# The last 128 dims of the first four x tiles: read as rows and turned on TensorE, in place of a transposing DMA

## The chip, the cores and the metric

The kernel runs on one core of one Trainium2 chip. The core has TensorE (PE: matmuls; PEld: its weight loads), VectorE (DVE), ScalarE (ACT), GpSimd (POOL) and SyncE (SP, which here only issues transfers), and 16 DMA engines that all transfers share. The metric is the device time of one execution in microseconds: 170.68 us is the median of 3 runs (170.39 to 171.07).

## What is computed

`x` is 2048 tokens of 448 dims, in bf16. The result is `g * a + (1 - g) * b`: a gated mix of a segmented attention with a memory (a) and of an MLP that mixes tokens (b).

```python
x = A_x                                                # (1, 2048, 448)
g = _sigmoid((x * gate_w).sum(-1, keepdims=True))
# a: 16 heads of 28 dims, 4 segments of 512 tokens
q, k, v = x @ wq, x @ wk, x @ wv
for s in range(4):
    logits = einsum('bhqd,bhkd->bhqk', qs, ks) * scale + mask
    a_dot = einsum('bhqk,bhkd->bhqd', softmax(logits), vs)
    a_mem = (phi(qs) @ M) / (phi(qs) @ z + 1e-06)      # phi(t) = t + 1 if t > 0 else exp(t)
    outs.append(sig(beta) * a_mem + (1 - sig(beta)) * a_dot)
    M, z = M + phi(ks).T @ vs, z + phi(ks).sum()
a = concat(outs) @ wo
# b: layernorm over dims, then a two-layer MLP along the token axis (2048 -> 1792 -> 2048)
h = layernorm(x)
u = gelu(einsum('bsd,sf->bdf', h, w1) + b1)
b = (einsum('bdf,fs->bds', u, w2) + b2).transpose(0, 2, 1)
return g * a + (1 - g) * b
```

## The kernel before

**x is held twice.** `xh` holds it as rows: 16 tiles of 128 tokens, 448 dims each, for the layernorm and, once normalised, as the moving operand of the MLP. `xT` holds it turned, with the dims on the partitions: 4 chunks of 128 dims by 2048 tokens, for the projections to q, k and v. The chunks begin at dims 0, 128, 256 and 320 (`C0`), so the third and the fourth overlap by 64 dims. `xT` comes from transposing DMAs on SP's queue: for each of four blocks of 512 tokens (`tc`) one transfer for chunks 0 to 2 (`dtx{tc}_0`) and one for chunk 3 (`dtx{tc}_1`). `xh` comes from four plain transfers of four tiles each (`ldx0`, `ldx4`, `ldx8`, `ldx12`).

**The projections come in pairs** (`pair`). A projection sums over the 448 dims: chunks 0, 1, and then chunk 2 and the upper half of chunk 3, or chunk 3 and the lower half of chunk 2. The two half chunks of a pair (64 rows each) go first, side by side in the array, in one operation `lo...`. For the first block of tokens the matmuls over chunks 0 and 1 are set apart as heads (`pra`, `prb`), so that they can run before chunks 2 and 3 are used.

**The order of the start, on TensorE:** nine warm-up matmuls (`warm`); a small transposition of the gate vector (`gtr`), which VectorE writes into a column of wv (`gw`); one more warm-up matmul; the eight heads of v of tiles 0 to 3 (`pra0` to `pra3` on chunk 0, `prb3` to `prb0` on chunk 1); the half chunks of v (`lot2`, `lot0`); the rest of v (`prt1`, `prt3`, `prt2`, `prt0`); the heads of k (`pra0_1` and on); and so on to the scores of the attention (`sc0_0`) and the MLP (`u`, `y`), which fill the rest of the run. VectorE copies the weights of k and q into padded form (`padk`, `padx`, `padq`, line 662) once they have landed, and empties some of the PSUM banks (`cpv`, `cpk`, `cpq`); ScalarE empties the others. `bns` (line 916) are the statistics of the layernorm.

**What sets the order:** `ORDER` is a table of names, one string for each engine; `Sched.plan` puts the operations on each engine in that order, and `Sched.finalize` makes semaphore waits of the dependences between them. Nothing moves at run time: an engine that waits holds up all that stands behind it on that engine. SP issues nearly all loads, one after another; ScalarE issues those of wv, of the last part of wk and a few small ones at the very start.

The line of the transposing DMA is 535, of the row loads 520, of the weight loads 525 and 529; 282 is the helper `mm` that issues the projections and the MLP, 973 the scores.

Of the kernel before, what the change touches and what calls it, by code (L numbers as in the profile page):

```python
# [297 lines left out]
def pool_cost(n):
# [6 lines left out]
    "PE": """  # L305
warm gtr@4 warm2 pra0@7 pra1@4 pra2@5 pra3@6 prb3 prb2 prb0 prb1 lot2 lot0 prt1 prt3 prt2 prt0 pra0_1 pra0_2 pra0_0
btr@7 lok0_0 lok0_2 prk0_0 prx0_3 prk0_2 prk0_1 prt7@4 prx1_3@5 prk1_2@6 lot6@7 lok1_2 loq0_0 loq0_2 prq0_2 prq0_0
prt6 prq1_2@4 prq0_2h prq1_1@5 prq1_2h@6 loq1_0@7 loq1_2 prq0_1 prq1_0 prk1_1@4 sc0_0 lok1_0@5 lot4@67 prk1_0 prt5
prt4 sc0_1 prk2_1@4 prx2_3@5 prk2_2@6 lok2_2 lok2_0@7 sc0_2 prk2_0 u1-0@6*5 u0-0@4 u1-5 u0-1*2 u2-0@5*3 sc0_3 u0-3
u2-3*2 u0-4*2 u3-0@7*2 u0-6 u2-5*2 u3-2 u1-6 sc0_4 u1-7 u0-7*6 u3-3 u0-13 u2-7 u3-4 u0-14*2 u1-8 sc1_0 u1-9*6 u2-8*2  # L310
u1-15 u2-10*4 u3-5*2 u4-0@4 u3-7*2 sc1_1 u5-0@6*2 u2-14 u5-2*2 u2-15 u3-9*6 u5-4 u3-15 u4-1*5 u5-5*2 pv1@5 u4-6*2
sc1_2 u4-8 u5-7*5 u4-9*4 u5-12 pv0@7 u5-13 sc1_3 u4-13*3 u6-0@5*3 u7-0@7 u6-3 u5-14 u6-4*2 u5-15 u6-6 sc1_4 u6-7
u7-1 u6-8*4 u7-2*2 u6-12 u7-4*3 u6-13*3 sc2_0 u7-7*7 pv2@4 u7-14*2 sc2_1 mst0@6 u8-0@4*2 prq2_1@5 prq2_0@7 loq2_0
sc2_2 u8-2*4 prq2_2@5 u8-6*4 prq2_2h@6 loq2_2 mem1 u8-10*2 u9-0@5 u8-12 u9-1*8 u8-13*2 u11-0@6 sc2_3 u9-9*3 pv3@7
u9-12 u8-15 u9-13*2 u11-1 u9-15 u11-2*4 sc2_4 u10-0@7*3 u11-6*6 u13-0@4 u10-3 pv4@5 sc3_0 u10-4*12 u11-12 u13-1
sc3_1 u13-2*3 u11-13*2 u13-5*2 pv5@5 u11-15 prt9@7 u13-7*4 sc3_2 lot8@5 u13-11*2 u12-0@6*5 prt8 u13-13*3 u12-5 sc3_3
lot10@57 u12-6*3 prt11 u12-9*7 prt10 sc3_4 mst1@7 prk3_1@4 pv6@6 prk3_0@7 lok3_0 sc4_0 prq3_1@5 prq3_0@7 wo0@6
loq3_0 lw0@4 sc4_1 wo1 pv7@5 prk3_2@6 wo3@7 lok3_2@4 lw2@5 sc4_2 wo2 prx3_3 y0-0@6*5 mem2 y0-5*9 prq3_2h@4 prq3_2@5
# [6 lines left out]
y10-10*2 y11-9*3 y10-12 y11-12*2 lw14@45 y10-13 wo14 wo15 wo12@7 y12-0@6*2 lw12@5 wo13 y13-0@4*4 y15-0@7 y13-4*2
y14-0@5*2 y13-6*4 y12-2 y14-2*2 y13-10 y14-4 y12-3*2 y13-11 y12-5*3 y14-5 y15-1 y12-8*3 y14-6*3 y13-12*2 y12-11*3
y14-9*5 y15-2*12 y15-0#1@4 y15-1#1 y15-2#1 y15-3#1 y15-4#1 y15-5#1 y15-6#1 y15-7#1 y15-8#1 y15-9#1 y15-10#1 y15-11#1
y15-12#1 y15-13#1""",
# [11 lines left out]
    "DVE": """  # L340
ob0 gw padk0 padx0 cpv3 padk1 padx1 padk2 padx2 padq0 padq1 b2c padq2 b1c padq3 cpk0_0 cpk0_2 mk0_0 bns3 bns1 bns0
phk0_0 bns2 bna1 bna3 bna2 bns7 bns9 bna0 bns5 bns10 vpe0 bns11 bns6 bna9 cpq1_0 bna7 bns4 bna6 gcol0 bna5 bna4 vpe4
nmr0 bna10 bns8 ln1 b1h ln2 bna8 cpk1_0 b1s mk0_1 bns13 bna11 phk0_1 nmr4 bns15 ln0 bna15 omgh vpe8 ln3 ln4 gh ln5
cpq2_3 bns12 bna12 bna13 bns14 ln6 mq1_1 bna14 nmr8 ln11 ln8 ln9 vpe12 ln10 ln7 omg0 nmr12 mg0 ln12 ln13 ln15 ln14
mq1_2 mg1 mg2 mo0 phq1_2 gvh0 garg0 phq1_1 garg1 mk0_2 gelu0 phk0_2 mq1_0 gvh2 gelu1 garg2 phq1_0 mk0_3 oc0 phk0_3
garg3 mq1_3 ta1 ta0 rec0 mk1_0 gelu2 oc1 gelu3 oa0 phk1_0 gvh5 gvh4 garg5 garg4 mk1_1 rec1 phk1_1 oa1 gelu4 gelu5
ta2 gvh6 gvh7 ot1 msta0 garg6 mstc0 mk1_2 phk1_2 rec2 phq1_3 garg7 cpq2_2 tm4 tm7 tm5 tm6 b2g0 eps6 gelu7 gelu6
mk1_3 eps4 phk1_3 oa2 ta3 mq2_0 phq2_0 gvh8 garg8 rec3 gcol1 eps7 garg9 mq2_2 ot2 ta4 gelu8 gelu9 rec4 ot0 oa3 omg1
mk2_0 mq2_1 phk2_0 phq2_1 garg10 ta5 gvh11 garg11 eps5 mk2_1 phk2_1 b2g1 om4 phq2_2 oa4 gelu11 ot3 gelu10 rec5 om5
gvh13 gvh12 msta1 garg12 oa5 garg13 ot4 ta6 cpk3_1 rec6 om6 ag0 oa6 ag1 ta7 gelu12 rec7 mq2_3 gelu13 phq2_3 mstc1  # L350
om7 oa7 tm8 tm9 tm10 tm11 cpq3_2 cpq3_2#1 ot5 mk2_2 eps8 eps9 eps11 gcol2 fin0 mk2_3 mq3_1 phk2_3 phk2_2 ta8 rec8
ot6 eps10 oa8 om8 ot7 phq3_1 oy8 fin1 fin3 ag4 ot8 mq3_0 phq3_0 ta9 rec9 omg2 fin2 om9 oa9 mq3_2 ta10 rec10 om10 ot9
ag7 fin5 mq3_3 phq3_2 oa10 ta11 rec11 msta2 phq3_3 oa11 mstc2 om11 tm12 tm13 tm14 tm15 ot11 ot10 cpv15 cpv14 eps13
fin4 ta12 eps15 gcol3 b2g2 eps12 omg3 rec12 oa12 fin6 ag8 om12 ta13 ot12 rec13 fin7 om13 oa13 o13 ot13 eps14 fin8
ag10 ta14 rec14 om14 oa14 ta15 rec15 om15 oa15 b2g3 fin9 ot14 ot15 fin11 fin10 fin13 fin12 fin14 fin15 fin15#1""",
# [23 lines left out]
def build_kernel(nc, X, WQ, WK, WV, WO, BETA, W1, B1, W2, B2, GW, OUT):  # L379
# [153 lines left out]
    def transpose_x(tc):  # L533
        for k, (c, n) in enumerate(((0, 3), (3, 1))):
            op("SP", lambda e, c=c, n=n: e.dma_start_transpose(
                xT[:, c : c + n, tc * 512 : tc * 512 + 512], x2[tc * 512 : tc * 512 + 512, C0[c] : C0[c] + 128 * n]),
               writes=[R_xT[tc][k]], name=f"dtx{tc}_{k}", dma=True, cost=1200 * n, nbytes=227000 * n, prio=(-3, -3, -1, 0)[tc])
# [294 lines left out]
    def do_gw():  # L832
        b = Bank()

        def gps():
            return bank(b)[:, 0:NCT]

        def fn(e):
            e.matmul(bank(b)[:, 0:3], gstage[:, :], ident[:, 0:5:2], start=True, stop=True, skip_group_check=True)
            return e.matmul(bank(b)[:, 3:4], gstage[:, :], ident[:, 5:6], start=True, stop=True, skip_group_check=True)  # L840
# [3 lines left out]
        op("DVE", lambda e: e.tensor_copy(wvx[:, :, D], gps()), use=(b,), reads=[bres(b)], writes=[R_gw], name="gw", cost=80,  # L844
           prio=P_BASE)
# [69 lines left out]
    def ln_stats(t):  # L915
        op("DVE", lambda e: e.bn_stats(st6[:, t, :], xh[:, t, :]), reads=[R_x[t]], writes=[R_st6[t]], name=f"bns{t}",  # L916
           cost=512, prio=P_PROJ - 10, rel=7500.0)
# [377 lines left out]
```

## Time and profile before

| | |
|---|---|
| median of 3 runs (range) | 170.68 us (170.39 to 171.07) |
| the profiled execution: its time; its span, first to last instruction | 170.68 us; 168.9 us |
| TensorE busy | 164.7 us (98%) |
| VectorE, ScalarE, GpSimd busy | 136.7 us (81%), 130.6 us (77%), 64.3 us (38%) |
| first matmul; first matmul of v; last matmul ends | 0.82; 5.21; in the microsecond from 166 to 167 |
| chain that ended last | TensorE 94%, a DMA 3% |
| DMA traffic | 25.44 MB, 151 GB/s mean |

A row of a timeline gives the start, the length and the engine, the line and the operation, out<-in, how many, and in brackets how long the engine had sat idle and what ended it. A matmul's record covers its whole way through the array; the next begins before it ends. So the spacing of the starts is what one costs. PEld rows show when the weights of a matmul are loaded, shortly before it starts. SPq and ACTq rows are the issue of transfers; the time to landing is counted from the start of the issue.

### The profile page before, as it was taken

The page shows a single profiled execution, that of the slowest core. Times are in us where ns is not written, and L with a number is a line of the kernel's source. Part 1 is how long each engine was busy: PE and PEld are TensorE (multiplying, and loading weights), DVE is VectorE, ACT ScalarE, POOL GpSimd, SP SyncE. Part 2 cuts the span into 40 slices and gives each one's busy share as a digit, 9 for nine tenths or more (in the row PEclk, how much of TensorE's full clock was granted, in tenths as well). Part 3 has the DMA queues.
Part 4 walks back from the last instruction along what each step waited for, and adds up shares of the span by engine and source line. Part 5 has one row for each costly group of instructions (what it writes and reads, how often), then busy time and mean ns, then how long its engine had stood idle before and what let it go on. Part 6 is the DMA issues. An engine that isn't in the chain of part 4 may idle for free.

```text
span 168.9 us, 4944 instructions
## 1 busy us (share of the span) xinstructions
PE 164.7 (98%) x2022; PEld 78.5 (47%) x2026; DVE 136.7 (81%) x321; ACT 130.6 (77%) x164; POOL 64.3 (38%) x100
## 2 busy tenths in 40 slices
PE   8999999999999999999999999999999999999994
PEld 2334444444554644544453454444454444564553
DVE  0088999877989989999999999999999978695042
ACT  0359999999999997999999998988985788604100
POOL 5000245260442524142177356445837355540000
PEclk9999999999999999999999999999999999999999
DMA  6998999888699945994337302328853129831202
GB/s 144 249 258 289 248 153 246 160 228 226 138 167 254 222 101 146 163 213 124 109 98 169 82 4 65 94 82 111 244 148 110 46 70 280 229 103 60 84 27 82
DMA packets 53974, 25.44 MB, mean 151 GB/s; under 512 B 18416, under 2 KB 53712, under 8 KB 53952
## 3 DMA queue, kind: packets, MB, share of 16 engines
q1 hardware_dynamic: 53160, 24.54, 61.2%
q10 hardware_dynamic: 792, 0.58, 1.7%
q8 instruction: 16, 0.26, 0.7%
q14 instruction: 6, 0.05, 0.1%
HBM read 18.82 MB, written 2.36 MB: 125 GB/s over the span
## 4 chain that ended last, share of the span: by engine, by line
PE 94%; DMA 3%; ACTq 1%; issue 1%; POOL 0%; DVE 0%; POOLq 0%
PE t L282 79%; PE t L973 8%; PE t L1003 5%; DMA t<-in_A_wv_dram 3%; PE t L856 1%; PE t L1076 1%; ACTq L525 1%; ACTq L546 0%; DVE t L1165 0%; POOL t L544 0%; POOL t L620 0%; POOL t L587 0%; POOL t L619 0%; POOL t L615 0%; POOLq L1280 0%
## 5 line engine op out<-in xcount | busy, mean ns | idle before, releaser
L282 PE MATMUL t<-t 128*32 128x448 bf16 (+9 forms) x1257 | 140.4, 352 | 1.0 <-issue 0.6
L282 PEld LDWEIGHTS t<-t 128*32 128x32 bf16 (+2 forms) x1261 | 63.7, 97 | 63.8 <-issue 15.3
L982 ACT ACTIVATE t<-t 128x2048 bf16<-128x2048 f32 x40 | 75.2, 1879 | 6.8 <-PE t L973 6.2
L985 POOL TENSOR_SCALAR_AFFINE_SELECT t<-t 128x512 bf16<-128x512 bf16 x64 | 43.3, 688 | 43.0 <-ACT t L982 40.0
L1040 POOL TENSOR_TENSOR t<-t 128x448 bf16<-128x448 f32 (+2 forms) x13 | 13.3, 1026 | 19.0 <-DVE t L1033 14.4
L1165 DVE SCALAR_TENSOR_TENSOR t<-t 128x448 bf16<-128x448 f32 (+2 forms) x17 | 10.7, 642 | 10.6 <-PE t L282 10.5
L973 PE MATMUL t<-t 28*128 28x512 bf16 (+3 forms) x256 | 15.8, 301 | 0.0
L1017 DVE STREAM_TRANSPOSE t<-t 128x512 f32<-128x512 f32 x16 | 11.3, 706 | 2.9 <-PE t L1003 2.7
L925 POOL TENSOR_TENSOR t<-t 128x4 f32<-128x4 f32 x4 | 4.2, 1054 | 23.4 <-DVE t L923 21.4
L1119 ACT ACTIVATE t<-t 128x448 bf16<-128x448 f32 x10 | 7.1, 732 | 7.6 <-PE t L282 7.6
L1003 PE MATMUL t<-t 128*32 128x512 bf16 (+3 forms) x256 | 11.5, 300 | 0.0
L1059 DVE STREAM_TRANSPOSE t<-t 128x512 bf16<-128x512 bf16 x16 | 10.9, 690 | 0.0
L973 PEld LDWEIGHTS t<-t 28*128 28x128 bf16 x256 | 4.4, 92 | 14.0 <-ACT t L982 7.7
L818 ACT ACTIVATE t<-t 128x448 bf16<-128x448 f32 x13 | 6.8, 546 | 4.2 <-PE t L282 4.2
L916 DVE BATCH_NORM_STATS2 t<-t 128x6 f32<-128x448 bf16 x16 | 9.3, 610 | 0.7 <-DMA t<-in_A_x_dram 0.7
L1145 DVE SCALAR_TENSOR_TENSOR t<-t 128x448 f32<-128x448 f32 x14 | 9.0, 649 | 0.7 <-ACT t L1140 0.6
L1003 PEld LDWEIGHTS t<-t 128*32 128x32 bf16 x256 | 6.7, 96 | 5.3 <-issue 0.7
L1137 ACT ACTIVATE t<-t 128x448 f32<-128x448 f32 x14 | 8.8, 638 | 0.1
L779 ACT ACTIVATE t<-t 128x512 bf16<-128x512 bf16 x12 | 7.6, 635 | 1.4 <-DVE t L736 1.4
L808 DVE SCALAR_TENSOR_TENSOR t<-t 128x512 bf16<-128x512 bf16 x12 | 8.5, 712 | 0.1
L1143 DVE TENSOR_SCALAR t<-t 128x448 f32<-128x448 f32 x10 | 6.5, 676 | 2.4 <-ACT t L1137 2.3
L1033 DVE SCALAR_TENSOR_TENSOR t<-t 128x448 f32<-128x448 f32 x12 | 8.4, 699 | 0.0
(76 smaller groups left out, 132.1 us busy)
## 6 DMA issues: line engine op xcount, KB each, us to landing
t<-in_B_w_dram SPq DMA_DIRECT2D x52, 256.0 KB, 3.9
t<-in_A_x_dram SPq DMA_DIRECT2D x4, 448.0 KB, 5.4
out_dram<-t SPq DMA_DIRECT2D x15, 112.0 KB, 2.0
t<-in_B_w_dram SPq DMA_DIRECT2D x8, 128.0 KB, 2.5
t<-in_A_wv_dram ACTq DMA_DIRECT2D x4, 112.0 KB, 4.1
t<-in_A_wq_dram SPq DMA_DIRECT2D x1, 336.0 KB, 4.8
spare_heads<-t SPq DMA_DIRECT2D x8, 32.0 KB
spare_heads<-t SPq DMA_DIRECT2D x16, 16.0 KB
```

The source lines that it names most:

```text
L282: last = e.matmul(out[q], w[:, q], x, skip_group_check=True, **kw)
L916: op("DVE", lambda e: e.bn_stats(st6[:, t, :], xh[:, t, :]), reads=[R_x[t]], writes=[R_st6[t]], name=f"bns{t}", cost=512, prio=P_PROJ - 10 ...
L973: last = e.matmul(bank(hl)[:, c0 : c0 + w], kT[r, hg, s * 512 + j * 128 : s * 512 + j * 128 + 128], qT[r, hg, s * 512 + 128 * j : s * 512 ...
L982: op("ACT", lambda e: e.activation(pslot(g), ps[:, 0:4, :], ACT.Exp, scale=SCALE), reads=R_bank[0:4], writes=[g.res], take=g, name=f"exp{p ...
L985: op("POOL", lambda e, c0=c0: e.affine_select(pslot(g)[:, :, c0 : c0 + 128], pslot(g)[:, :, c0 : c0 + 128], pattern=[[0, 4], [1, 128]], co ...
L1003: last = e.matmul(bank(cb)[32 * ((hl + hg) % 4) : 32 * ((hl + hg) % 4) + 32, 128 * j : 512], vaug[:, 4 * s + j, 32 * h : 32 * h + 32], psl ...
L1017: dv(lambda e: e.transpose(tt[:, ia, :], bank(cb)[:, 0:512]), [bres(cb)], [R_tt[ia]], "ta", 630, use=(cb,))
L1040: return e.tensor_tensor(dst, part(n3[0]), part(n3[1]), op=ALU.add)
L1059: dv(lambda e: e.transpose(oT[:, hg, s * 512 : s * 512 + 512], o), [R_ob[hg]] + ([R_obx] if hg else []), qres(hg, s), "ot", 635)
L1137: op("ACT", lambda e: e.activation(gg[:, q, :], bank(b)[:, 0:D], ACT.Square, bias=b1s[:, ft : ft + 1], scale=math.sqrt(GC)), **buse(b), re ...
L1145: op("DVE", lambda e: e.scalar_tensor_tensor(gg[:, q, :], gg[:, q, :], 1.0, vh[:, q, :], op0=ALU.add, op1=ALU.mult), reads=[R_gg[q], R_vh[ ...
L1165: op("DVE", lambda e: e.scalar_tensor_tensor(outst[:, p, c0:c1], bank(b)[:, 0 : c1 - c0], omg[:, T : T + 1], ag(T)[:, c0:c1], op0=ALU.mult ...
```

## The change

The transposing DMA of chunk 3 of the first 512 tokens (`dtx0_1`) is gone; those of the other blocks stay. In its place on SP's queue, right behind `dtx0_0`, a plain transfer `ldxl` reads dims 320 to 447 of the first four x tiles as rows into `xh` (128 partitions, 4 tiles, 128 dims: runs of 256 bytes), and `ldx0` later reads only dims 0 to 319. Four matmuls against the identity (`xtl`) turn the four 128x128 pieces into PSUM bank 2, and one copy on VectorE (`cpxl`, 128x512) writes them to `xT`. The statistics of tiles 0 to 3 now also wait for `ldxl`. What is computed is the same.

```diff
-dtx0_0 dtx0_1 ldwk0@0 ldwk1 ldwq0@1 ldwqb dtx1_0 dtx1_1 ldx0 ldx4 ldx8 ldbeta ldw1_0_0 dtx2_0 ldx12 dtx2_1 ldw1_0_1
+dtx0_0 ldxl ldwk0@0 ldwk1 ldwq0@1 ldwqb dtx1_0 dtx1_1 ldx0 ldx4 ldx8 ldbeta ldw1_0_0 dtx2_0 ldx12 dtx2_1 ldw1_0_1
...
+    R_xl = R("xl")
+
+    def load_x(eng, t0, n, c0=0, c1=D, writes=None, name=None):
+        op(eng, lambda e: e.dma_start(xh[:, t0 : t0 + n, c0:c1], xv[:, t0 : t0 + n, c0:c1]),
+           writes=writes or R_x[t0 : t0 + n], name=name or f"ldx{t0}", dma=True, cost=500, nbytes=n * 256 * (c1 - c0), prio=-3)
...
-        for k, (c, n) in enumerate(((0, 3), (3, 1))):
+        for k, (c, n) in enumerate(((0, 3), (3, 1))[: 2 if tc else 1]):
...
+    load_x("SP", 0, 4, C0[3], D, [R_xl], "ldxl")
     transpose_x(0)
...
-    load_x("SP", 0, 4)
+    load_x("SP", 0, 4, 0, C0[3])
...
+    def last_dims():
+        def fn(e):
+            for t in range(4):
+                last = e.matmul(bank(2)[:, t * 128 : t * 128 + 128], xh[:, t, C0[3] : D], ident[:, :], start=True, stop=True,
+                                skip_group_check=True)
+            return last
+
+        op("PE", fn, reads=[R_xl, R_ident], writes=[R_bank[2]], name="xtl", mode="f", cost=4 * pe_cost(128), prio=P_PROJ - 1)
+        op("DVE", lambda e: e.tensor_copy(xT[:, 3, 0:512], bank(2)[:, 0:512]), reads=[R_bank[2]], writes=[R_xT[0][1]],
+           name="cpxl", cost=dve_cost(512), prio=P_BASE)
```

The table of orders differs in little else: some bank numbers of the first v tiles, and a few neighbours exchanged further on. TensorE issues four matmuls more than before (2030 for 2026), which are those of `xtl`.

TensorE's start, before; "waits" names the semaphores (s_dma_u2 is that of `dtx0_1`, s_dma_u5 and s_dma_u6 those of the last two parts of wv; the second row of line 282 that has waits is `prb3`, the third `lot2`):

```order
L651 MATMUL t<-const-bfloat16-1.0 128x512
L282 MATMUL t<-t 128x449 [waits s_DVE,s_dma_u3,s_dma_u1]
L282 MATMUL t<-t 128x449 x3
L282 MATMUL t<-t 128x449 [waits s_dma_u4]
L282 MATMUL t<-t 128x449 x3
L282 MATMUL t<-t 128x449 [waits s_dma_u6,s_dma_u5,s_dma_u2]
L282 MATMUL t<-t 128x449 x7
L282 MATMUL t<-t 128x512 [waits s_DVE]
```

The same place of the changed kernel (s_dma_u1 is now `ldxl`):

```order
L282 MATMUL t<-t 128x449 [waits s_DVE,s_dma_u3,s_dma_u2]
L282 MATMUL t<-t 128x449 x3
L282 MATMUL t<-t 128x449 [waits s_dma_u4]
L282 MATMUL t<-t 128x449 x3
L854 MATMUL t<-t 128x128 [waits s_dma_u1]
L854 MATMUL t<-t 128x128 x3
L282 MATMUL t<-t 128x449 [waits s_dma_u6,s_dma_u5,s_DVE]
L282 MATMUL t<-t 128x449 x7
L282 MATMUL t<-t 128x512 [waits s_DVE]
```

The four turning matmuls stand behind the eight heads and before `lot2`; `lot2` no longer waits for a transposing DMA, but for VectorE, whose copy waits for these four.

VectorE's start, before (line 844 is `gw`, 662 the pads of k, 820 `cpv3`):

```order
L586 MEMSET t 128x256
L844 CAST t<-t 128x4 [waits s_PE]
L662 COPY t<-t 128x2x14x28 [waits s_dma_u7]
L662 COPY t<-t 128x2x14x4
L820 CAST t<-t 128x16x28 [waits s_PE]
```

And of the changed kernel (lines are shifted by 4; 859 is `cpxl`):

```order
L590 MEMSET t 128x256
L848 CAST t<-t 128x4 [waits s_PE]
L859 CAST t<-t 128x512 [waits s_PE]
L666 COPY t<-t 128x2x14x28 [waits s_dma_u7]
L666 COPY t<-t 128x2x14x4
L824 CAST t<-t 128x16x28 [waits s_PE]
```

The copy stands ahead of the first pads of k, which wait for the load of wk.

More of the change, by code (lines that the diff above doesn't have):

```diff
@@ L305 @@
     "PE": """
[L306 to L315, printed above, removed]
@@ L316 @@
-sc3_1 u13-2*3 u11-13*2 u13-5*2 pv5@5 u11-15 prt9@7 u13-7*4 sc3_2 lot8@5 u13-11*2 u12-0@6*5 prt8 u13-13*3 u12-5 sc3_3
-lot10@57 u12-6*3 prt11 u12-9*7 prt10 sc3_4 mst1@7 prk3_1@4 pv6@6 prk3_0@7 lok3_0 sc4_0 prq3_1@5 prq3_0@7 wo0@6
+warm gtr@4 warm2 pra0@5 pra1@4 pra2@6 pra3@7 prb3 prb2 prb0 prb1 xtl lot2 lot0 prt1 prt3 prt2 prt0 pra0_1 pra0_2
+pra0_0 btr@5 lok0_0 lok0_2 prk0_0 prx0_3 prk0_2 prk0_1 prt7@4 prx1_3@5 prk1_2@6 lot6@7 lok1_2 loq0_0 loq0_2 prq0_2
+prq0_0 prt6 prq1_2@4 prq0_2h prq1_1@5 prq1_2h@6 loq1_0@7 loq1_2 prq0_1 prq1_0 prk1_1@4 sc0_0 lok1_0@5 lot4@67 prk1_0
@@ new lines @@
+prt5 prt4 sc0_1 prk2_1@4 prx2_3@5 prk2_2@6 lok2_2 lok2_0@7 sc0_2 prk2_0 u1-0@6*5 u0-0@4 u1-5 u0-1*2 u2-0@5*3 sc0_3
+u0-3 u2-3*2 u0-4*2 u3-0@7*2 u0-6 u2-5*2 u3-2 u1-6 sc0_4 u1-7 u0-7*6 u3-3 u0-13 u2-7 u3-4 u0-14*2 u1-8 u2-8 sc1_0
+u1-9*6 u2-9 u1-15 u2-10*4 u3-5*2 u4-0@4 u3-7*2 sc1_1 u5-0@6*2 u2-14 u5-2*2 u2-15 u3-9*6 u5-4 u3-15 u4-1*5 u5-5*2
+pv1@5 u4-6*2 sc1_2 u4-8 u5-7*5 u4-9*4 u5-12 pv0@7 u5-13 sc1_3 u4-13*3 u6-0@5*3 u7-0@7 u6-3 u5-14 u6-4*3 u5-15 sc1_4
+u6-7 u7-1 u6-8*4 u7-2*2 u6-12 u7-4*3 u6-13*3 sc2_0 u7-7*7 pv2@4 u7-14*2 sc2_1 mst0@6 u8-0@4*2 prq2_1@5 prq2_0@7
@@ L324 @@
 y8-12*2 y9-4 sc7_4 lw10 y9-5*5 pv14@5 y10-0@6*7 y9-10*2 pv15@5 y11-0@7 y10-7 y11-1*3 y10-8*2 y9-12*2 y11-4*5
[L325 to L327 removed]
+y10-10*2 y11-9*3 y10-12 y11-12*2 lw14@45 y10-13 wo14 wo15 wo12@7 y12-0@6*2 lw12@5 wo13 y13-0@4*6 y14-0@5*2 y13-6*4
+y12-2 y15-0@7 y14-2*2 y13-10 y14-4 y12-3*2 y13-11 y12-5*3 y14-5 y15-1 y12-8*3 y14-6*3 y13-12*2 y12-11*3 y14-9*5
+y15-2*12 y15-0#1@4 y15-1#1 y15-2#1 y15-3#1 y15-4#1 y15-5#1 y15-6#1 y15-7#1 y15-8#1 y15-9#1 y15-10#1 y15-11#1
 y15-12#1 y15-13#1""",
@@ L340 @@
     "DVE": """
[L341 to L345, printed above, removed]
@@ L351 @@
[L351 to L355, printed above, removed]
+ob0 gw cpxl padk0 padx0 cpv3 padk1 padx1 padk2 padx2 padq0 padq1 b2c padq2 b1c padq3 cpk0_0 cpk0_2 mk0_0 bns3 bns1
@@ L356 @@
+rec8 ot6 eps10 oa8 om8 ot7 phq3_1 oy8 fin1 fin3 ag4 ot8 mq3_0 phq3_0 ta9 rec9 omg2 fin2 om9 oa9 mq3_2 ta10 rec10
+om10 ot9 ag7 fin5 mq3_3 phq3_2 oa10 ta11 rec11 msta2 phq3_3 oa11 mstc2 om11 tm12 tm13 tm14 tm15 ot11 ot10 cpv15
+cpv14 eps13 fin4 ta12 eps15 gcol3 b2g2 eps12 omg3 rec12 oa12 fin6 ag8 om12 ta13 ot12 rec13 fin7 om13 oa13 o13 ot13
+eps14 fin8 ag10 ta14 rec14 om14 oa14 ta15 rec15 om15 oa15 b2g3 fin9 ot14 ot15 fin11 fin10 fin13 fin12 fin14 fin15
+fin15#1""",
     "POOL": """
@@ L915, in ln_stats @@
     def ln_stats(t):
-        op("DVE", lambda e: e.bn_stats(st6[:, t, :], xh[:, t, :]), reads=[R_x[t]], writes=[R_st6[t]], name=f"bns{t}",
+        op("DVE", lambda e: e.bn_stats(st6[:, t, :], xh[:, t, :]), reads=[R_x[t]] + ([R_xl] if t < 4 else []), writes=[R_st6[t]], name=f"bns{t}",
            cost=512, prio=P_PROJ - 10, rel=7500.0)
@@ L1178, in build_kernel @@
     do_gw()
+    last_dims()
     def pairs(tc, *specs):
```

28 lines of the change are left out of this document (17 added, 11 removed).

## The prediction

> **What bounds the kernel now.** I read the page first, then busy time by stretches, then the chain of waits and the timelines of the first 12 us, then the transfers. The page says that TensorE is the bound, and the stretches say that it is so without a break:
>
> ```profile
> PE 164.7 (98%) x2022; PEld 78.5 (47%) x2026; DVE 136.7 (81%) x321; ACT 130.6 (77%) x164; POOL 64.3 (38%) x100
> PE 94%; DMA 3%; ACTq 1%; issue 1%; POOL 0%; DVE 0%; POOLq 0%
> ```
> ```profile
> 7.50:20.70 13.20, 13.12 (x75) 5.73 (x76) 10.95 (x34) 10.27 (x27) 1.04 (x1) 1.00 1.04 272
> 27.00:60.00 33.00, 33.00 (x473) 16.20 (x465) 28.86 (x72) 32.28 (x38) 13.88 (x21) 1.00 0.87 197
> 120.00:166.50 46.50, 46.50 (x605) 23.73 (x603) 33.03 (x63) 23.96 (x23) 17.57 (x24) 1.00 0.41 121
> ```
>
> The first busy time in a row is TensorE's: 13.12 of 13.20 us behind the start, 33.00 of 33.00, 46.50 of 46.50. So a microsecond that TensorE loses at the start comes out at the end, unless TensorE later loses one less somewhere else. The start in detail, by the chain of waits, then TensorE and its weight loads:
>
> ```profile
> 2.96 4.43 DMA t<-in_A_wv_dram
> 7.39 0.14 issue
> 7.52 1.42 PE t L282 x8
> ```
> ```profile
> 5.21 2.02 PE L282 MATMUL t<-t 128*128 128x449 bf16 x8
> 7.52 2.90 PE L282 MATMUL t<-t 64*128 64x449 bf16 x14 [0.29 <-DMA t<-in_A_wv_dram]
> ```
> ```profile
> 3.34 0.15 PEld L651 LDWEIGHTS t<-const-bfloat16-1.0 128*128 128x128 bf16 x1 [0.28 <-issue]
> 3.77 0.15 PEld L651 LDWEIGHTS t<-const-bfloat16-1.0 128*128 128x128 bf16 x1 [0.28 <-issue]
> ...
> 5.92 0.87 PEld L282 LDWEIGHTS t<-t 128*128 128x128 bf16 x5 [0.22 <-issue]
> 7.49 0.14 PEld L282 LDWEIGHTS t<-t 64*128 64x128 bf16 x4 [0.70 <-DMA t<-in_A_x_dram]
> 8.01 0.49 PEld L282 LDWEIGHTS t<-t 128*128 128x128 bf16 x4 [0.37 <-issue]
> 8.95 0.98 PEld L282 LDWEIGHTS t<-t 128*128 128x128 bf16 x6 [0.45 <-DVE t L662]
> ```
>
> The eight heads of v end at 5.21 + 2.02 = 7.23. `lot2` starts at 7.52, so the hole that the edit is about is 0.29 us wide. Two transfers end it nearly together. The chunk-3 transposition is issued at 2.24 (right behind the first one) and lands 5.0 later, at 7.24; the last part of wv is issued at 2.96 and lands 4.43 later, at 7.39:
>
> ```profile
> L535 SPq DMA_TRANSPOSE t<-in_A_x_dram x1: 1254/1254/1254, 2.2 to 2.2; - x1
> t<-in_A_x_dram SPq DMA_TRANSPOSE x1, 5.0
> t<-in_A_wk_dram SPq DMA_DIRECT2D x1, 224.0 KB, 4.9
> t<-in_A_wv_dram ACTq DMA_DIRECT2D x2, 112.0 KB, 4.5
> ```
>
> With the transposition away and the rest unmoved, `lot2` could not start before wv at 7.39: the wait that is removed is worth at most 0.29 us and, if wv lands as before, nothing.
>
> **What is removed.** One transposition of 1.25 us of SP's issue time; the row transfer in its place should take about what other plain ones do:
>
> ```profile
> 0.79 2.70 SPq L535 DMA_TRANSPOSE t<-in_A_x_dram  x2
> 3.55 1.08 SPq L525 DMA_DIRECT2D t<-in_A_wk_dram  x2
> 5.68 3.98 SPq L535 DMA_TRANSPOSE t<-in_A_x_dram  x2
> ```
>
> 1.08 / 2 = 0.54 us. So everything behind it on SP (wk, wq, the next transpositions, x rows, the first w1) is issued 1.25 - 0.54 = 0.7 us earlier. The traffic falls too: `ldx0` reads 128 KB less, just what `ldxl` reads, so the transposition's 128 KB are saved outright. Its packets run in the slices from 4 to 6 us, at the lowest rates of the start:
>
> ```profile
> DMA packets 1037, 0.29 MB, mean 290 GB/s; under 512 B 986, under 2 KB 1037, under 8 KB 1037
> DMA packets 290, 0.13 MB, mean 131 GB/s; under 512 B 195, under 2 KB 290, under 8 KB 290
> ```
>
> (The first row is the slice 3 to 4, the second 5 to 6.) I cost this relief at nothing by itself, since TensorE is full behind 7.5; it is only worth what it shortens waits, below.
>
> **When the rows land.** 128 KB, issued at about 2.24, 512 packets of 256 bytes behind the 1536 of the first transposition. At the 986 short packets per us of the slice 3 to 4 they take 0.5 us, at the 195 of the slice 5 to 6 they take 2.6 us. Counted from 4.0, where the first transposition's packets are about done, and with the 1.2 us from 6.0 to 7.24 that the removed one took from its last packets to its landing, that is 5.7 to 7.8. By the 4.5 us of 112 KB of wv it is 6.7. They are needed when the heads let go of the array, at 7.23 less the overlap of two matmuls. I take "in time"; the late end is a rival.
>
> The Trainium skill, "DMA: Bandwidth & Descriptors", Specifications, says that pieces under 512 bytes do not reach line rate, because a read-modify-write is done for them. The slice 3 to 4 speaks against a large effect here: 986 short packets went through at 290 GB/s, though for transposed data. By the page the 128 KB would cost like 256 KB or more, which is the late end again.
>
> **What is added in front of `lot2`.** Two steps that nothing covers, since `lot2` and all behind it wait on TensorE's one queue.
>
> ```profile
> L282 PE MATMUL t<-t 128*128 128x256 bf16 x12 | 1.8, 273 | 0.0
> L887 PE MATMUL t<-t 128*128 128x30 bf16 x1 | 0.2, 178 | 0.0
> L282 PEld LDWEIGHTS t<-t 128*128 128x128 bf16 x96 | 8.7, 98 | 11.0 <-issue 3.3 <-DVE t L662 0.4
> ```
> ```profile
> 4.89 0.18 DVE L844 CAST t<-t 128x4 bf16<-128x4 f32 x1 [3.71 <-PE t L840]
> 8.43 0.47 DVE L662 COPY t<-t 128x784 bf16<-128x784 bf16 x2 [3.36 <-DMA t<-in_A_wk_dram]
> 8.81 0.62 DVE L820 CAST t<-t 128x448 bf16<-128x448 f32 x1
> ...
> 11.33 0.69 DVE L736 CAST t<-t 128x512 bf16<-128x512 f32 x1
> ...
> 13.79 1.68 DVE L916 BATCH_NORM_STATS2 t<-t 128x6 f32<-128x448 bf16 x3 [0.70 <-DMA t<-in_A_x_dram]
> ```
>
> (1) The turning matmuls. Warm matmuls of 448 or 449 columns start 0.19 us apart (the five loads from 5.92 take 0.87), so the last head, whose record of 0.35 ends at 7.23, starts at 6.88 and the first `xtl` can start at 7.07. Four of 128 columns: below, four times 0.053 (512 columns cost 0.216 warm, a quarter is 0.054); above, four weight loads of 0.098. The last one's way through the array lies between the 0.178 of 30 columns and the 0.273 of 256: 0.22. The last ends between 7.45 and 7.58; I take 7.54. (2) The copy. A cast of 128x512 from PSUM takes 0.69. It starts 0.04 after the matmul (the small cast at 4.89, after a matmul that ends at 4.85), and a matmul's weight load follows a VectorE result by 0.11 (from 4.89 + 0.18 = 5.07 to the heads' first load at 5.18), the matmul itself by 0.03 more. So `lot2` starts at 7.54 + 0.04 + 0.69 + 0.14 = **8.41, 0.89 later than before** (0.80 to 0.93).
>
> **What is paid back.** First, at 8.95 the weight load for the heads of k waits for the pads of wk (0.45 before it, of which a spacing of 0.19 less a load of 0.10 is usual, and some is the four loads that came early). Without this wait the matmul would follow the last of v (8.01 + 0.03 + 4 x 0.19 = 8.80) instead of starting at 8.98: 0.18. In the changed kernel TensorE comes there at 9.69; wk, issued 0.7 earlier, lands by 8.45 - 0.7 = 7.75 and the pads (0.47) are done behind the copy at 8.27 + 0.47 = 8.74. So 0.18 comes back, 0.71 is left. VectorE's `cpv3` and the later pads move with TensorE, and stay as close to it as before. Second, at 24.16:
>
> ```profile
> 23.51 0.40 PE L973 MATMUL t<-t 28*128 28x384 bf16 x8
> 24.16 2.64 PE L282 MATMUL t<-t 128*128 128x512 bf16 x13 [0.26 <-issue]
> 26.73 0.40 PE L973 MATMUL t<-t 28*128 28x256 bf16 x8
> 27.07 3.09 PE L282 MATMUL t<-t 128*128 128x512 bf16 x15
> ```
> ```profile
> 18.10 1.18 SPq L535 DMA_TRANSPOSE t<-in_A_x_dram  x1
> t<-in_A_x_dram SPq DMA_TRANSPOSE x1, 6.0
> ```
>
> From scores to projections takes 27.07 - 26.73 = 0.34 where nothing is late, here 0.65: 0.31 is a wait, and it ends when the chunk-3 transposition of the third block lands (18.10 + 6.0 = 24.10). TensorE will come 0.7 later and that transfer not later than before, so this 0.31 comes back too. VectorE's own idle 0.70 before 13.79, for `ldx0`, takes up its lateness (the smaller `ldx0` is issued earlier). I find no other wait of TensorE for a load: 13.12 of 13.20 us are busy from 7.5 to 20.7, and none is left from 27 on.
>
> **Sum:** 0.89 - 0.18 - 0.31 = +0.40 us. The profiled execution took 170.68, which is also the median: **171.1 us**, +0.23%. A measurement here can tell about 0.5% (0.85 us) from no change, so this counts as the same.
>
> **Rivals.**
>
> (a) *The bubble stays whole.* If VectorE, with 10.95 us of work in 13.20, and the chain of bank releases behind it take the 0.89 without giving any back (the wait at 24.16 being that of an evacuation after all): 171.6, just past the 0.5%. For it: ScalarE and VectorE are nearly full from 22 to 60 us. Against it: the landing at 24.10 fits the start at 24.16 to a few hundredths. Decides: whether the pause before the projections at about 24.8 shrinks to 0.34.
>
> (b) *The rows land late* (slower). `ldxl` of short pieces lands after the heads, and `xtl` waits. It decides from a landing at 7.07 on, each 0.1 us later costing 0.1. The 256 KB loads of the same start are a bound:
>
> ```profile
> t<-in_B_w_dram SPq DMA_DIRECT2D x2, 256.0 KB, 5.8
> ```
>
> 2.24 + 5.8 = 8.04, 0.97 late: 171.08 + 0.97 = 172.0. Against it: at its place the queue carries only the first transposition.
>
> (c) *The pause drops TensorE's clock* (slower). The rows of the warm-up show it: loads 0.43 apart at 3.34 and 3.77 for 512 columns, against 0.216 later, so half speed. If a pause of 0.9 us sent it back for as long as the first ramp (0.82 to about 5.9, the heads from 5.92 being fast), half of 5 us is lost, 2.5: 173.6. A pause of 0.29 does nothing, by the spacing behind 8.01; none of 0.9 is in the trace. The Trainium skill, "TensorE: Matmul & The Clock Gate", What's actually happening, wants an idle window of about 3.4 us for that, which speaks against (c).
>
> (d) *The relief of the queues wins* (faster). Every load of the first 25 us comes 0.7 to 1.2 us earlier; if TensorE hides more waits for loads than its rows show, they come back. To be 0.5% faster, 0.89 + 0.85 = 1.7 us must be found, and the visible waits are 0.18 + 0.31; if as much again is hidden between records and 0.3 at each end, 170.3, still the same by the bound.
>
> (e) *The edit does nothing* because wv is last anyway: then no copy would be exposed, and 170.7. The order speaks against it: `lot2` waits for the copy.
>
> **Chances.** Forecast 0.57 (170.8 to 171.4); (a) 0.17, half of it past 0.5%; (b) 0.11; (c) 0.03; (d) 0.09, of which 0.05 past 0.5%; (e) 0.03. Slower: 0.085 + 0.11 + 0.03 = 0.23 with rounding; faster 0.05; same 0.72. The range from 170.3 to 171.9 takes in the forecast, (a), (e) and most of (d), and leaves out (b), (c) and the fast tail of (d).
>
> **What will show it.** In the changed profile: `xtl` (line 854) starting near 7.07 and not after a DMA; the cast of line 859 near 7.6, 0.69 long; the first 64-row matmul near 8.4 with VectorE as its releaser; the load for the heads of k 0.7 later than 8.95 and without a wait for line 666; the pause between scores and projections at about 24.9 at 0.34 instead of 0.65; and from there a constant lag of 0.4 to the end. It would be wrong if `xtl` waits for the x rows, if spacing behind 8.4 is 0.4, or if the lag at 27 is over 0.9 or below zero.

## The result, and the profile after

| | before | changed |
|---|---|---|
| median of 10 executions each (us) | 170.70 (170.12 to 171.07) | 171.46 (171.18 to 171.85) |
| ratio, with its 95% interval | | 1.0053 (1.0037 to 1.0068) |
| profiled execution: time / span (us) | 170.68 / 168.9 | 171.84 / 170.1 |

The change costs about half a per cent: the interval leaves out 1, and it lies across the 0.5% of the forecast. The median is 0.36 above the forecast of 171.1, inside the range of 170.3 to 171.9 and just outside the likeliest case's own range (170.8 to 171.4). The ten executions fall into two groups, six from 171.18 to 171.51 and four from 171.82 to 171.85. The profiled one is of the upper group; a second profiled execution of the same kernel, with a time like those of the lower group (171.43), stands below. Medians are over all executions of a run; ratios leave out the few in which the clock was visibly lower.

The summary of the page, after:

```profile
PE 164.2 (97%) x2026; PEld 78.5 (46%) x2030; DVE 137.4 (81%) x322; ACT 130.4 (77%) x164; POOL 63.7 (37%) x100
PE 93%; DMA 3%; SPq 1%; DVE 1%; issue 0%
```

TensorE is still the bound; what is new is that SP and VectorE stand in the chain. The chain of waits, after (start, length, what; two stretches of it):

```profile
2.21 5.66 DMA t<-in_A_x_dram
...
7.92 0.41 PE t L854 x4
...
8.35 0.70 DVE t L859
...
9.10 2.71 PE t L282 x14
...
11.87 2.51 PE t L282 x13
...
22.27 0.33 PE t L988 x4
...
25.01 0.33 PE t L988 x8
25.34 2.59 PE t L282 x13
...
149.63 18.07 PE t L282 x175
```

And the same places of the chain before, behind the rows that the prediction shows (wv landing at 7.39, `lot2` at 7.52):

```profile
10.43 2.73 PE t L282 x14
...
20.84 0.33 PE t L973 x4
...
23.58 0.33 PE t L973 x8
...
24.16 2.64 PE t L282 x13
...
148.46 18.07 PE t L282 x175
```

Read as lags of the changed kernel: `lot2` starts 9.10 - 7.52 = 1.58 later; the work behind its 14 matmuls 11.87 - 10.43 = 1.44 later; at 22.27 it is 1.43; at the projections 25.34 - 24.16 = 1.18; near the end 149.63 - 148.46 = 1.17, and the times differ by 171.84 - 170.68 = 1.16. So the whole loss arises ahead of `lot2`, 0.14 is paid back at the pads of k and 0.25 at the pause before the projections, and from there the lag is constant. That is the form that the forecast gave it. Its size at the start is not that of the forecast: 1.58 instead of 0.89.

TensorE's timeline at the start, after (the idle time before a row and what ended it stand in brackets):

```profile
4.93 1.68 PE L282 MATMUL t<-t 128*128 128x449 bf16 x8
7.92 0.40 PE L854 MATMUL t<-t 128*128 128x128 bf16 x4 [1.30 <-DMA t<-in_A_x_dram]
9.10 2.71 PE L282 MATMUL t<-t 64*128 64x449 bf16 x14 [0.79 <-DVE t L859]
```

The heads of v are done at 4.93 + 1.68 = 6.61, and TensorE then stands idle for 1.30 us until the x rows land at 2.21 + 5.66 = 7.87. The rows, not the heads, start the turning matmuls. In the second profiled execution, the chain of waits reads:

```profile
2.23 5.16 DMA t<-in_A_x_dram
...
7.43 0.41 PE t L854 x4
...
7.87 0.70 DVE t L859
...
8.62 2.72 PE t L282 x14
```

Here the rows land at 7.39, and `lot2` starts at 8.62. Both times `lot2` follows the landing by 1.23. The 0.48 between the two landings is close to the distance between these two times (171.84 - 171.43 = 0.41). That the landing makes the two groups is likely, but one profile of each doesn't show it. Finally two loads of the first profiled execution, one of wk issued at 2.84 and the last part of wv issued at 2.93 (KB each, us from issue to landing):

```profile
t<-in_A_wk_dram SPq DMA_DIRECT2D x1, 224.0 KB, 6.0
t<-in_A_wv_dram ACTq DMA_DIRECT2D x1, 112.0 KB, 5.1
```

Before, they took 4.9 and 4.43; in the second profiled execution of the change 5.2 and 5.0. So wk, though issued 0.7 earlier, lands at 2.84 + 6.0 = 8.84 here, later than the 3.55 + 4.9 = 8.45 of before. Which transfers slow each other down is tried below, by the run that holds back SP's later loads.

### The profile page after: what moved, and what is told of

Its sections match the earlier page's. It is cut to its first block, busy times and chain, and to the rows that moved or that the text cites. A ratio compares the mean times of both kernels' runs of the same rounds, so it can differ in the third digit from the quotient of the medians.

```text
span 170.1 us, 4953 instructions
## 1 busy us (share of the span) xinstructions
PE 164.2 (97%) x2026; PEld 78.5 (46%) x2030; DVE 137.4 (81%) x322; ACT 130.4 (77%) x164; POOL 63.7 (37%) x100
## 4 chain that ended last, share of the span: by engine, by line
PE 93%; DMA 3%; SPq 1%; DVE 1%; issue 0%
PE t L282 78%; PE t L988 8%; PE t L1018 5%; DMA t<-in_A_x_dram 3%; PE t L871 1%; SPq L538 1%; PE t L1091 1%; DVE t L859 0%; PE t L854 0%; DVE t L1180 0%; PE t L902 0%
## 5 line engine op out<-in xcount | busy, mean ns | idle before, releaser
L1000 POOL TENSOR_SCALAR_AFFINE_SELECT t<-t 128x512 bf16<-128x512 bf16 x64 | 42.8, 680 | 44.5 <-ACT t L997 41.5
L1160 DVE SCALAR_TENSOR_TENSOR t<-t 128x448 f32<-128x448 f32 x14 | 9.5, 682 | 0.8 <-ACT t L1155 0.7
L1048 DVE SCALAR_TENSOR_TENSOR t<-t 128x448 f32<-128x448 f32 x12 | 8.4, 698 | 0.0
L1165 DVE SCALAR_TENSOR_TENSOR t<-t 128x448 bf16<-128x448 f32 x14 | 8.4, 614 | 0.0
```

The costliest lines, as they stand in the source:

```text
L1000: op("POOL", lambda e, c0=c0: e.affine_select(pslot(g)[:, :, c0 : c0 + 128], pslot(g)[:, :, c0 : c0 + 128], pattern=[[0, 4], [1, 128]], co ...
L1160: op("DVE", lambda e: e.scalar_tensor_tensor(gg[:, q, :], gg[:, q, :], 1.0, vh[:, q, :], op0=ALU.add, op1=ALU.mult), reads=[R_gg[q], R_vh[ ...
```

## One number that orders all runs

In all but three of the profiled executions, the span less the start of `lot2` is nearly the same:

| kernel | `lot2` | span | difference |
|---|---|---|---|
| before | 7.52 | 168.9 | 161.4 |
| changed, the two profiled executions | 9.10, 8.62 | 170.1, 169.6 | 161.0, 161.0 |
| e1 (rows loaded, nothing turned), e5 (nothing loaded), e9 (identity turned) | 7.76, 8.03, 7.90 | 168.7, 169.0, 168.9 | 160.9, 161.0, 161.0 |
| e3 (chain alone), e8 (rows on ACT) | 8.07, 9.15 | 169.1, 170.2 | 161.0, 161.1 |
| e11 (other transposition earlier) | 7.46 | 168.4 | 160.9 |

So an experiment on the start can be read from one row, the start of `lot2`, plus 161.0; the kernel before alone carries 0.4 more, which any later start gets back. The spans are given to 0.1. The three that don't follow are e2 (rows first on SP) and e4 (whole rows), where TensorE ran at half speed, and e10, where later loads were held back. A profiled execution need not be a typical one: that of e9 is the fastest of its twelve, and that of e5 is 0.43 slower than its median.

## The experiments

The theory behind them: the loss has two parts, the chain of four matmuls, a copy and two handovers that nothing covers (the forecast's +0.4), and rows that land too late (rival b). The rivals to it: that the chain itself costs more than forecast, that the earlier loads on SP cost time, and that the transposition taken away was worth something.

**The chain alone.** The kernel before, with all transfers as they were; four matmuls of the identity and a 128x512 copy into memory that nothing uses yet, which `lot2` waits for.

```diff
+        op("PE", fn, reads=[R_ident], writes=[R_bank[2]], name="xtl", ...)
+        op("DVE", lambda e: e.tensor_copy(uT[:, 0:2, 0:256], bank(2)[:, 0:512].rearrange("p (a b) -> p a b", a=2)),
+           reads=[R_bank[2]], writes=[R_scr, R_uT[0], R_uT[1]], name="cpxl", ...)
-                 x=..., need=rx + R_wv + [R_gw],
+                 x=..., need=rx + R_wv + [R_gw] + ([R_scr] if t < 4 else []),
```

> The kernel before with its chunk-3 transposition kept, plus four 128x128 matmuls of the identity and a copy of 128x512 on VectorE that lot2 waits for, so that only the turning and the copy are added and no transfer is changed; the copy's result is not used. Theory: lot2 at 8.41 (0.89 later), 0.18 and 0.31 come back, lag 0.40: 171.1. Rival (bubble stays whole): 171.6. Rival (the turning costs nothing and the transfers are all of it): 170.7.

171.07 against 170.73, ratio 1.0020 (1.0006 to 1.0033). TensorE's timeline of this kernel:

```profile
5.21 1.75 PE L282 MATMUL t<-t 128*128 128x449 bf16 x8
6.80 0.39 PE L851 MATMUL t<-t 128*128 128x128 bf16 x4
8.07 2.72 PE L282 MATMUL t<-t 64*128 64x449 bf16 x14 [0.88 <-DVE t L856]
```

`lot2` starts 1.27 after the first turning matmul (forecast 8.41 - 7.07 = 1.34), and the kernel loses 0.34 (forecast 0.40). The chain is what the forecast said it is, and it is less than half of the 0.76 between the two medians of the change.

**The change without its wait for the rows.** As the changed kernel, rows loaded at the same place, but the turning matmuls read the identity instead of them and wait for no transfer; the last 128 dims of the first 512 tokens are so left out of the computation.

```diff
-                last = e.matmul(bank(2)[...], xh[:, t, C0[3] : D], ident[:, :], ...)
+                last = e.matmul(bank(2)[...], ident[:, :], ident[:, :], ...)
-        op("PE", fn, reads=[R_xl, R_ident], ...)
+        op("PE", fn, reads=[R_ident], ...)
```

> The changed kernel with all its transfers, but the four matmuls turn the identity, which is there from the start, and not the rows: they don't wait for the row load, so chunk 3 of the first 512 tokens holds ones and zeros and not x. It takes the landing of the rows out of the chain and leaves the turning and the copy in. Theory (the forecast's chain of 0.4 plus about 0.4 for rows that land after the heads): 171.0 to 171.1, lot2 at 8.0 to 8.1 or with wv if that is later. Rival (earlier issue of the other loads costs the extra 0.4, whatever the rows do): 171.4 to 171.5.

170.96 against 170.64 for the kernel before on the same chip, ratio 1.0018 (1.0004 to 1.0032). Its chain of waits:

```profile
6.85 0.24 PE t L854 x4
7.11 0.70 DVE t L859
...
7.90 2.72 PE t L282 x14
```

The changed kernel again, on this chip:

> The changed kernel once more, beside the others on the same chip: 171.3 to 171.6. Theory: the rows land at another time in this execution (in the kernel without turning they landed at 7.2 behind the same transfers, against 7.87 here before), and the start of lot2 follows the landing by 1.2.

171.32, ratio 1.0045 (1.0029 to 1.0061). So with the rows' transfer running but not waited for, the loss is 0.32, near the chain's 0.34; with the wait it is 0.68. **The lateness of the rows is worth 0.36**, on the same chip and with the same transfers. The chain measured by itself and this lateness add up to 0.34 + 0.36 = 0.70, against 0.76 between the medians of the change.

**Neither chain nor transposition.** Two kernels leave the last 128 dims of the first 512 tokens at zero: one keeps the changed kernel's transfers, rows among them, the other is the kernel before with the transposition dropped and nothing in its place.

```diff
-... prb2 prb0 prb1 xtl lot2 lot0 ...
+... prb2 prb0 prb1 lot2 lot0 ...
-        op("DVE", lambda e: e.tensor_copy(xT[:, 3, 0:512], bank(2)[:, 0:512]), reads=[R_bank[2]], ...)
+        op("DVE", lambda e: e.memset(xT[:, 3, 0:512].bitcast(U32), 0), ...)
```

> The changed kernel with its row load, but without the four turning matmuls and their copy: chunk 3 of the first 512 tokens is set to zero on VectorE ahead of the gate column, so this part of x does not enter q, k and v of these tokens. Theory (the loss is the exposed chain of landing, turning and copy): lot2 starts when wv lands, and that is 7.4 to 8.05; time 170.4 to 171.0, clearly below the 171.46 of the changed kernel. Rival (the loss is on the transfer side: wv and wk land later since SP issues its loads earlier): lot2 at 8.05 or later behind wv, wk waits grow too, 171.2 to 171.5.

```diff
-dtx0_0 dtx0_1 ldwk0@0 ldwk1 ldwq0@1 ldwqb ...
+dtx0_0 ldwk0@0 ldwk1 ldwq0@1 ldwqb ...
+    op("DVE", lambda e: e.memset(xT[:, 3, 0:512].bitcast(U32), 0), writes=[R_xT[0][1]], name="cpxl", ...)
```

> The kernel before without the chunk-3 transposition of the first 512 tokens and with nothing in its place: that part of xT is set to zero on VectorE at the start, so these 128 dims do not enter q, k and v of these tokens. It bounds what the removal can be worth. Theory: lot2 waits for wv alone, at 7.1 to 7.4, worth 0 to 0.3 us: 170.4 to 170.7. Rival (the relief of the queues is worth more): 169.8 to 170.2.

The first takes 170.62, ratio 0.9992 (0.9981 to 1.0002); the second 170.40, ratio 0.9989 (0.9975 to 1.0002). Neither can be told from before. Why, the chains of waits say, the first kernel's

```profile
2.93 4.70 DMA t<-in_A_wv_dram
...
7.76 2.72 PE t L282 x14
```

and the second's:

```profile
2.96 4.93 DMA t<-in_A_wv_dram
...
8.03 2.72 PE t L282 x14
```

With nothing left to wait for but wv, `lot2` starts at 7.76 and 8.03, later than the 7.52 of before. The last part of wv is issued at 2.93 to 2.96 as ever, but takes 4.70 and 4.93 instead of 4.43: wk and wq are issued earlier on SP, and the run with SP's loads held back, below, shows that this counts. In the second kernel's profiled execution `lot2` is therefore 0.5 later, of which the 0.4 above comes back. Its median execution is 0.43 faster; by the 161.0 of the table its `lot2` would start near 7.6 (an estimate). So the wait that the edit removes was worth little: the intervals leave room for a gain of 0.2 to 0.25%, 0.3 to 0.4 us, and for none, and the forecast's own bound was "at most 0.29 us and, if wv lands as before, nothing".

The slice from 5 to 6 us of the second kernel:

```profile
DMA packets 359, 0.29 MB, mean 290 GB/s; under 512 B 35, under 2 KB 359, under 8 KB 359
```

Before, this slice had 131 GB/s; in the run with the chain alone, which keeps the transposition, it has 141.

**SP's later loads held back.** The changed kernel, in which the first load of wk, and so everything behind it on SP, waits until the rows have landed.

```diff
-               writes=[r[k]], name=f"ld{name}{k}", ...)
+               reads=[R_xl] if name == "wk" and k == 0 else [], writes=[r[k]], name=f"ld{name}{k}", ...)
```

> The changed kernel, but SP issues wk and all that stands behind it only when the rows have landed, so that the rows share the DMA engines with the first transposition and ScalarE's small loads and wv alone. It will be slower as a whole (wk lands some 5 us later than before, near 12); what counts is when the rows and wv land. Theory (the rows are late because the DMA engines stand half idle for about 1 us behind the transposition): landing still 7.0 to 7.9, with the slice 4 to 5 us still under 220 GB/s. Rival (the rows and wv are late because wk and wq, issued 0.7 us earlier, take their share): rows by 6.5 and the last part of wv by 6.8.

The last part of wv and the rows in this kernel:

```profile
t<-in_A_wv_dram ACTq DMA_DIRECT2D x1, 112.0 KB, 3.9
t<-in_A_x_dram SPq DMA_DIRECT2D x1, 128.0 KB, 4.5
```

The rows land 4.53 after their issue instead of 5.16 to 5.66, at 6.74, and the last part of wv at 2.93 + 3.9 = 6.83 instead of about 8. So what SP issues right behind the rows (wk, wq, then the next transpositions) delays both by 0.6 to 1.2 (one profiled execution); which of these loads does it is not separated. Of the two expectations it is the rival's that comes near (6.5 and 6.8). Here the rows are in time, and the heads, which end at 7.62, hold back the turning: `lot2` starts at 8.63, no earlier than in the second profiled execution of the change. The kernel takes 172.19, ratio 1.0088 (1.007 to 1.0107; two executions), because wq then comes late:

```profile
8.18 3.71 DMA t<-in_A_wq_dram
...
12.35 2.36 PE t L282 x11
```

The Trainium skill, "DMA: Bandwidth & Descriptors", Issuing engines are not separate DMA queues, says that transfers share the same 16 DMA engines and interleave, whichever engine issued them. These rows agree: what SP issues moves the landing of what ACT issued.

**Another place for the rows.** `ldxl` first on SP, ahead of the transposition:

```diff
-dtx0_0 ldxl ldwk0@0 ...
+ldxl dtx0_0 ldwk0@0 ...
```

> The changed kernel with the row load issued ahead of the transposition of chunks 0 to 2 on SP. Theory (the rows land at 7.87 because they stand behind that transposition): they land near 3.1 (issue at 0.79 plus the 2.3 of the first wv part), the turning starts when the heads let go, the heads start up to 0.6 later (5.2 to 5.5); lot2 8.4 to 8.7, the lag from 26 us on 0.4 to 0.7, time 171.0 to 171.3. Rival (short 256-byte pieces are slow wherever they stand): landing 5.7 us behind the issue, 6.5, and the first transposition 1 us or more later, heads at 6 or later: 171.6 to 172.2.

177.62, ratio 1.0368 (1.0326 to 1.0411): both expectations fell, the slower one by over 5 us. The transfers issued up to 5 us, then the chain of waits, then the weight loads:

```profile
t<-in_A_x_dram SPq DMA_DIRECT2D x1, 128.0 KB, 2.9
t<-in_A_x_dram SPq DMA_TRANSPOSE x1, 7.0
```
```profile
1.31 7.03 DMA t<-in_A_x_dram
...
8.38 3.18 PE t L282 x8
...
12.78 4.58 PE t L282 x14
```
```profile
9.11 0.15 PEld L282 LDWEIGHTS t<-t 128*128 128x128 bf16 x1 [0.23 <-issue]
9.48 0.15 PEld L282 LDWEIGHTS t<-t 128*128 128x128 bf16 x1 [0.22 <-issue]
```

The rows themselves are there early, 2.9 after issue, where 112 KB of wv issued at the same time took 2.4. So the 256-byte pieces alone don't account for the 5.2 and 5.7 of the change. But the transposition behind them takes 7.0 to land, where it took 3.7 to 3.9 as the first on the queue. The heads start at 8.38, and TensorE runs them at half speed: loads 0.37 apart for 449 columns, which take 0.19 in the forecast's rows, and the 14 matmuls of `lot2` take 4.58 instead of 2.72.

The rows on ACT's queue ahead of the last parts of wv, and turned between the two halves of the heads, where the copy is covered:

```diff
-ldwv0 ldgw ldwv1 ldwv2 ...
+ldwv0 ldgw ldxl ldwv1 ldwv2 ...
-... pra3@7 prb3 prb2 prb0 prb1 xtl lot2 ...
+... pra3@7 xtl prb3 prb2 prb0 prb1 lot2 ...
-dtx0_0 ldxl ldwk0@0 ...
+dtx0_0 ldwk0@0 ...
```

> The changed kernel with the row load issued by ScalarE between the gate vector and the second part of wv, and the turning matmuls put between the heads on chunk 0 and those on chunk 1, so that the copy runs beside the latter. Theory (the exposed chain is the loss): the copy is hidden, lot2 waits for the last part of wv, issued 0.5 later than in the changed kernel and landing near 8.2; 170.6 to 171.0. Rival (the row load on ScalarE's queue delays the second part of wv by 0.5 or more and with it the heads): 171.2 to 171.6. Rival (a plain transfer ahead of or beside the first transposition slows that, as when the rows were first on SP): heads at 6 or later, over 172.

171.91, ratio 1.0083 (1.0063 to 1.0103), 0.9 above the 170.6 to 171.0 that the theory gave. Its chain of waits:

```profile
3.50 5.52 DMA t<-in_A_wv_dram
...
9.15 2.72 PE t L282 x14
```

The rows land 4.5 after an issue at 1.97, at 6.47; turning and copy are done well before wv lands and cost nothing. But wv's last part is issued at 3.50 instead of 2.93 and takes 5.52 instead of 4.43, and `lot2` is as late as in the slower profiled execution of the change. The chain can be hidden, and then wv decides.

**The rows as whole rows.** `ldxl` reads all 896 bytes of each row at the same place, 448 KB, and the later `ldx0` goes:

```diff
-    load_x("SP", 0, 4, C0[3], D, [R_xl], "ldxl")
+    load_x("SP", 0, 4, 0, D, [R_xl] + R_x[0:4], "ldxl")
-    load_x("SP", 0, 4, 0, C0[3])
```

> The changed kernel with whole rows of the first four tiles (896-byte pieces, 448 KB) loaded at the place of the 256-byte pieces (128 KB), and no later load of their other dims. Theory A (the pieces are late since they are short): as many pieces, each at line rate, land no later than 7.4, and the time falls to 171.0 to 171.2. Theory B (they are late since everything behind the transposition waits for a gap in which the DMA engines are half idle, and then goes by its bytes): the landing moves to 8.2 to 8.8, time 171.8 to 172.3.

173.97, ratio 1.0192 (1.0158 to 1.0227). Chain of waits, the transfers of the slice 4 to 5, and busy time by stretches (TensorE, weight loads, VectorE, ScalarE, GpSimd, then the granted clock, the DMA share and GB/s):

```profile
2.22 6.61 DMA t<-in_A_x_dram
...
8.87 0.41 PE t L853 x4
...
10.05 4.19 PE t L282 x14
```
```profile
DMA packets 173, 0.14 MB, mean 136 GB/s; under 512 B 23, under 2 KB 173, under 8 KB 173
```
```profile
9.00:10.00 1.00, 0.27 (x4) 0.09 (x2) 0.69 (x2) 0.00 (x0) 0.00 (x0) 0.88 1.61 310
11.00:12.00 1.00, 1.00 (x3) 0.34 (x4) 0.12 (x1) 0.00 (x0) 0.00 (x0) 0.50 1.11 244
13.00:14.00 1.00, 1.00 (x6) 0.39 (x4) 0.23 (x3) 0.97 (x6) 0.00 (x0) 0.91 0.68 154
```

Two things. The slice 4 to 5 has a low rate with almost no short pieces (23 of 173 packets under 512 bytes, 136 GB/s; before, it had 189). And the rows land 6.61 after issue, at 8.83, just past the range of theory B; the time is over its range because of the clock. TensorE waits 1.44 and then 0.78 for the copy, and its clock is granted at 0.50 from 10 to 13. Taken from the 0.88 and the 0.91 of the rows at both ends, half speed lasted from about 9.76 to 13.18, that is 3.4 us (an estimate). This is rival (c), seen after a longer pause than that of the change.

**The other wait alone.** The kernel before, with the third block's second transposition issued before the load of the x rows of tiles 12 to 15, so that it lands ahead of the projections that wait for it:

```diff
-... ldw1_0_0 dtx2_0 ldx12 dtx2_1 ldw1_0_1
+... ldw1_0_0 dtx2_0 dtx2_1 ldx12 ldw1_0_1
```

> The kernel before, with the chunk-3 transposition of the third block issued ahead of the last load of x rows and not behind it. It tests the second payback: if TensorE's pause before the projections at 24.16 was a wait for that landing, it goes: 23.9 instead of 24.16, and the kernel is 0.2 to 0.3 us faster than before (170.4). Rival (the pause has another cause, a bank that is let go late): no change, 24.16 and 170.65; or a loss, if the last tiles' statistics, now 0.6 us later, hold VectorE up.

170.37 against 170.75, ratio **0.9976 (0.9957 to 0.9994)**. The chain of waits:

```profile
7.46 2.77 PE t L282 x14
...
23.40 0.33 PE t L973 x8
23.73 2.59 PE t L282 x13
```

From these scores to the projections it is 23.73 - 23.40 = 0.33; before it was 24.16 - 23.58 = 0.58 in the same view. The pause that pays back part of every later start is a wait for this transposition, and it can be had without losing anything first. This kernel is faster than both: 0.4 below before on the same chip, and about 1.1 below the 171.46 of the changed one.

## Why the prediction came out as it did

It was right on the sign, on where the time is lost (TensorE's queue ahead of `lot2`) and on where it is paid back. Its sum was 0.36 short, mainly through one term, the landing of the rows. One of its own signs of being wrong came: `xtl` waits for the x rows. The lag at 27 (28.31 - 27.13 = 1.18 in the first profiled execution, 0.70 in the second) is over its bound of 0.9 in the first.

The accounts of the two profiled executions close: the turning starts 0.85 and 0.36 later than the 7.07 of the forecast, the chain behind it is 0.16 and 0.15 shorter than its 1.34, and 0.10 less is paid back. That makes 0.79 and 0.31 on top of the 0.40, and the measured lags near the end are 1.17 and 0.72.

- **"I take 'in time'"** for the landing of the rows is the step that failed. The forecast's own range for the landing was 5.7 to 7.8; measured are 7.39 and 7.87, at its late end and just past it, against the 7.07 at which they were needed, and the 6.7 by which it judged them. Rival (b), given 0.11, is what happened, at a smaller price than its 172.0: each 0.1 of lateness did cost 0.1, and the lateness was 0.3 to 0.8. The removed transposition took 5.0 to its landing; the rows in its place take 5.0 to 5.7 in the four profiled executions with these same transfers (the change twice, e1, e9). That 512 short packets replace a transposition of the same 128 KB didn't make them quicker. Nor does a run show the doubled cost that the forecast worked out for pieces of 256 bytes as its late end: first on SP they took 2.9, and with SP's later loads held back 4.5.
- **The need moves too.** The forecast fixed the heads' end at 7.23, from one execution. Over the profiled executions of this case they end between 6.61 and 5.21 + 2.41 = 7.62 (the run with SP's loads held back) where they start near 5 us, since full speed comes at another moment each time: the loads of the heads reach the short spacing of about 0.19 at 5.9 before and at 6.7 with SP's loads held back, and have it from the start in the profiled execution of the change. There the heads end at 6.61, not 7.23. A margin measured against one execution's 7.07 was too generous.
- **The relief, costed "at nothing by itself",** is a small loss at the start: the last part of wv took 4.70 to 5.1 instead of 4.43, and wk 5.2 and 6.0 in the change instead of 4.9. So wk did not land by 7.75, as the forecast took it, but at 8.05 and 8.84. The copy ends at 8.56 and 9.04, after that, and so hides it. Rival (d), a gain from the earlier queues, is bounded by the kernel with nothing in the transposition's place: its interval leaves at most 0.25%, and its gain can't be told from none. In the change itself the later wv lies in the shadow of the chain; the rows are delayed by the same competition.
- **The chain of two steps** was well sized: 1.18 to 1.27 from the first turning matmul to `lot2` against 1.34. The copy of 0.70 is the greatest part, as forecast. The matmuls took 0.41 instead of 0.47.
- **Paid back:** 0.14 + 0.25 = 0.39 instead of 0.18 + 0.31 = 0.49. Both places are the right ones: the changed kernel shows no wait for the pads, and 25.34 - 25.01 = 0.33 at the pause. That the second is the wait for the transposition is shown by the run that moved it; rival (a) falls. The 0.31 was read from a timeline, of which the view of the chain shows 0.25.
- **Rival (c)** did not happen in the change: with pauses of 1.30 and 0.79 the 14 matmuls behind them take 2.71, as ever. But a near neighbour shows it. In the run with whole rows, half speed for about 3.4 us follows pauses of 1.44 and 0.78 with 0.41 of work between. The Trainium skill, "TensorE: Matmul & The Clock Gate", What's actually happening, gives an idle window of about 3.4 us for that. Read as a length of the pause, as the forecast read it, the trace disagrees: from the end of the heads at 8.87 - 1.44 = 7.43 to the first matmul of `lot2` at 10.05 are only 2.6 us, 0.4 of them busy. What is 3.4 long in this trace is the slow stretch itself.
- **The slow slices** from 4 to 6 us were put down to the transposition's packets. For the slice 5 to 6 that fits: the profiled executions that keep the transposition have 131, 141 and 175 GB/s there (before, e3, e11), and the eight without it whose first transposition stands first on SP have 207 to 302. For the slice 4 to 5 it does not fit: with whole rows it has 136, with nothing in the transposition's place 219, and before 189. What slows that slice stays open.
- **"Same"** had 0.72, slower 0.23: the ratio of 1.0053 is just over the 0.5% line, with an interval that reaches to both sides of it.
